# Top-1 routing: tokens routed at the start of the step behind their choice, and one sequence routed in two halves

## The chip, the cores and the metric

The kernel runs on one core of a Trainium2 chip. The metric is the device time of one execution in microseconds (us), the median of several runs. TensorE is called PE here, VectorE DVE, ScalarE ACT, GpSimd POOL and SyncE SP.

## The reference

The program computes attention with a local window and a few global keys, and sends its output as tokens through a layer of eight experts, of which each token uses one.

```python
# attention: B=4 sequences, H=8 heads, S=768 tokens, D=64; n_global=8, n_local=96
scores = q @ k.T / sqrt(D) - slope[h] * dist        # kept where local or global, else -1e9
a = exp(scores - max); a = a / (sum(a) + 1e-9)
x = (a @ v) as (B*S, H*D)                           # 3072 tokens x 512
# experts: E=8, w1 512x1024, w2 1024x512
logits = x @ w_gate; e = argmax(logits); p = softmax(logits)[e]
out[token] = p * (relu(x[token] @ w1[e]) @ w2[e])
```

## The kernel before, in words

**Tiles and order.** A sequence has six blocks of 128 tokens (NBLK = 6), so there are N = 24 blocks. The attention is a software pipeline of 24 steps, steps(n). Step n computes the scores of block n, the values of block n - 1, the sums and transposes of block n - 2, and the division of block n - 3 by its sums. The program writes every engine's instructions down in the order of the Python calls; each engine works through its own list in order, and a recorder (class Flow) puts in the semaphore waits that the data need. There is no scheduler: what is called first stands first in its engine's queue.

**What a step holds**, with the lines of the profile:

- scores (PE, L491, 32 matmuls, 16 in a sequence's first block), into PSUM banks 0 to 3.
- weigh (DVE, L501, or L503 in a first block), twice: adds the bias to half of the scores. exponent (ACT, L509), twice. both (POOL, L515 or L517), twice: adds the two key tiles for the row sums, into one of three buffers es, and reads the exponent's buffer e, of which there are two.
- values (PE, L528, 32 matmuls) and the copy of its result (ACT, L531).
- sums (PE, L543, 24 small matmuls: row sums and router logits), copied by ACT (L545); tokens_x and tokens_u (PE, L550, L553): transposes that bring a block back to one token per partition.
- normal (DVE, L562 to L566: four operations) takes the reciprocal of the sums and makes the logits; rows (DVE, L571) writes the tokens.
- q_in and k_in (PE, L475, L467): transposes of the tiles for step n + 2, copied by ACT (L477, L469). k_in writes bank 3, which weigh of the second half reads.
- copies of the global keys and values over the first rows of an older tile (POOL, L1096 and L1152, in step 22 ACT, L1094 and L1120).

**Routing.** When a sequence's six blocks have logits, at the end of steps 8, 14 and 20, choose (DVE, L584 to L588, and an exponent of ACT, L589) finds each token's expert, and gates (DVE, L594 to L598) its weight. In the next step counts (PE, L605 to L610: twelve small matmuls with a triangle and with ones) counts ahead of each token those of the same expert, and slots (DVE, L618 to L623) makes of it the token's row in a DRAM buffer, xg_dram, that has a region for each expert. base_e carries the counts on from sequence to sequence. Each block's tokens then go to their rows in one indirect DMA that POOL issues (scatter, L627). The calls wait in a list, scat; at the end of every step one is taken from it, and in the last sequence, from its fourth block on, all that are left (six, in step 21). The fourth sequence is routed later, inside the first group of the experts.

**Behind it.** At the end of step 21, load_x(0) loads expert 0's rows of the first three sequences (SP, L779 and L788); it waits until these sequences' scatters have landed. early_counts (DVE, L733 to L743 and three more) fixes expert 0's number of rows and so the form of its matmuls. marks and x_in (DVE, L795, L806) use what load_x brought. The experts' matmuls (PE, L842) follow; their up and down products use seven block products instead of eight, and w_sums (DVE, L710 to L713) makes the sums of weights that this takes: eight operations for expert 0, one at the end of each step from 13 to 20.

Of the kernel before, what the change touches and what calls it, by code (L numbers as in the profile page):

```python
# [15 lines left out]
I32 = mybir.dt.int32  # L16
AF = mybir.ActivationFunctionType
ALU = mybir.AluOpType
AX = mybir.AxisListType
# [305 lines left out]
class Attention:  # L325
# [9 lines left out]
    GW, LW, P, E = 32, 97, 128, 8  # L335
# [238 lines left out]
                            ALU.mult)  # L574


    def choose(self, b):

        f, k, V = self.f, self.keep, self.f.dve
        xr, lg = self.xr[b % 2], self.lg[b % 2]  # L580
        shape = [128, self.NBLK, self.E]
        sh, cand = self.small[:, 0], self.small[:, 1]
        top = self.top
        V.tensor_reduce(top, lg, AX.X, ALU.max)  # L584
        V.tensor_tensor(sh, lg, top.unsqueeze(2).to_broadcast(shape), ALU.subtract)
        V.scalar_tensor_tensor(cand, sh, 0.0, k["rev8"][:].unsqueeze(1).to_broadcast(shape), ALU.is_ge, ALU.mult)
        V.tensor_reduce(top, cand, AX.X, ALU.max)
        V.tensor_tensor(k["oh"][:], cand, top.unsqueeze(2).to_broadcast(shape), ALU.is_equal)  # L588
        f.act.activation(sh, sh, AF.Exp)  # L589

    def gates(self, b):
        f, k, V = self.f, self.keep, self.f.dve
        xr, sh, se = self.xr[b % 2], self.small[:, 0], self.se
# [3 lines left out]
        V.tensor_copy(out=xr[:, :, 513:514].bitcast(I32), in_=k["tokid"][:].unsqueeze(2))  # L597
        V.tensor_scalar(k["tokid"][:], k["tokid"][:], self.S, None, ALU.add)  # L598

    def counts(self, bank):  # L600
        f, k, E, NB = self.f, self.keep, self.E, self.NBLK
        oh, n = k["oh"], self.NBLK * self.E
        flat = oh[:].rearrange("p u e -> p (u e)")
# [9 lines left out]
    def slots(self, b, bank):  # L613
        f, k, V, E = self.f, self.keep, self.f.dve, self.E
        n = self.NBLK * E
        pr = self.psum[:, bank, 384:384 + n + E]
        rk = self.small[:, 2]
        V.tensor_tensor(rk, pr[:, 0:n].rearrange("p (u e) -> p u e", e=E),  # L618
                        k["base_e"][:].unsqueeze(1).to_broadcast([128, self.NBLK, E]), ALU.add)
        V.tensor_tensor(k["base_e"][:], k["base_e"][:], pr[:, n:n + E], ALU.add)  # L620
        V.tensor_tensor(rk, rk, k["oh"][:], ALU.mult)
        V.tensor_reduce(self.slot, rk, AX.X, ALU.add)
        V.tensor_copy(out=k["slot_i"][:, b % 2, :], in_=self.slot)  # L623

    def scatter(self, b, u):
        k = self.keep
# [8 lines left out]
class Experts:  # L635
# [10 lines left out]
    P, E, CAP, LATE, COMMON = 128, 8, 512, 128, 208  # L646
# [329 lines left out]
def kernel(  # L976
# [26 lines left out]
    NB = NTOK // P - 1  # L1003
# [24 lines left out]
    ident, iota_p, col, before, ones, rev8, ebase, base_e, tokid = (  # L1028
        keep[nm] for nm in ("ident", "iota_p", "col", "before", "ones", "rev8", "ebase", "base_e", "tokid"))
# [7 lines left out]
    with ExitStack() as stack:  # L1037
# [6 lines left out]
        f = Flow(tc)  # L1044
# [5 lines left out]
        N, V = at.N, f.dve  # L1050
        O, U, T0, T1, SK = 4, 5, 6, 7, 3
# [14 lines left out]
        at.loads(3)  # L1066

        scat, routed = [], {}
        tokens = [[f"xs{b}.{u}" for u in range(NBLK)] for b in range(B)]
        w0 = ex.w_pieces(0)  # L1070
        w0_sums = ex.w_sums(0, True) + ex.w_sums(0, False)
# [15 lines left out]
        def steps(n):  # L1087
            b, i = divmod(n, NBLK)
            at.scores(n)
            if i < NBLK - 1 and i >= 1:  # L1090

                first_k = at.kt[n % 3][:, :, 0:32], at.kg
                if n == N - 2:
                    f.act.copy(*first_k)  # L1094
                else:
                    f.pool.tensor_copy(out=first_k[0], in_=first_k[1])  # L1096
            if n >= 5 and w0:
                w0.pop(0)()
            if n == 0:
                kk, qq = at.k_in(1, O), at.q_in(1, U)  # L1100
                f.pool.tensor_copy(out=at.kg, in_=at.kt[0][:, :, 0:32])
            if n + 4 < N:
                at.loads(n + 4)
            if n + 3 < N:
                at.load_v(n + 3)
            at.weigh(n, 0)
            at.exponent(n, 0)
            if n == 0:
                kk()
                qq()  # L1110
            if n >= 3:
                at.normal(n - 3, U)
            first_v = None
            if n >= 1:
                values_part(n)
                bb, ii = divmod(n - 1, NBLK)
                if 1 <= ii < NBLK - 1:
                    first_v = at.v[(n - 1) % 6][0:32].rearrange("p h d -> p (h d)"), at.vg[bb % 2]
                    if n == N - 2:
                        f.act.copy(*first_v)  # L1120
            if n - 4 in routed:
                at.counts(T1)
# [18 lines left out]
            if n + 2 < N:  # L1141
# [12 lines left out]
            if us:  # L1154
                us()
                at.tokens_u(n - 2, U)
            if kk:
                qq()
                kk()
                if (n + 2) % NBLK == 0:  # L1160
                    f.pool.tensor_copy(out=at.kg, in_=at.kt[(n + 2) % 3][:, :, 0:32])
            if n == 1:
                V.tensor_scalar(before[:], col[:], iota_p[:, 0:1], None, ALU.is_gt)
                V.memset(ones[:], 1.0)
                V.tensor_copy(out=base_e[:], in_=ebase[:])
# [73 lines left out]
        def group(p):  # L1239
# [6 lines left out]
            def at_(i, *fns):  # L1246
                todo.setdefault(i, []).extend(fns)
# [41 lines left out]
            if g == 0:  # L1289
# [4 lines left out]
                pieces = ex.w_pieces(1)  # L1294
# [7 lines left out]
                        fn()  # L1302
                    ex.load_x(1, last)

                at_(2, lambda: at.normal(N - 1, U), lambda: at.choose(B - 1), *pieces[4:])
                at_(4, lambda: at.counts(U), lambda: at.gates(B - 1))
                at_(5, lambda: at.slots(B - 1, U))
# [468 lines left out]
```

## Time and profile before

| What | Value |
|---|---|
| Median of 3 runs | 517.89 us (516.78 to 520.77) |
| The profiled execution's own time | 517.95 us |
| Its span, first to last instruction | 516.1 us |
| Mean granted clock of PE | 0.985 |
| PE busy from step 20's values to step 22's scores (134.36 to 148.38 us) | 13.30 us |
| PE busy from step 22's values to step 23's scores (148.38 to 161.94 us) | 8.81 us, granted clock 0.77 |
| Indirect DMAs of L627, issue time | 24, mean 1030 ns |

The busy times come from a table of stretches: each row gives a stretch's length, then for each engine its busy time and the number of its instructions, then PE's granted clock, the share of the DMA engines' time and the rate in GB/s. A line of a timeline gives the start, the length, the engine, the line of the program, the operation, what it writes and reads, how many are merged, and, in brackets, how long the engine stood idle before it and what ended that. In a list of waits the numbers are the total in us, how often, and the longest.

Single scatters start at 71.8 us (end of step 9) and follow one per step until 139.4 us; six stand together at 147.6 to 155.1 us, and six more, those of the fourth sequence, at 182.9 to 190.7 us.

### The profile page before, as it was taken

The numbers are of one execution on the slowest core, as the hardware profiler recorded it, in microseconds if no ns is written. First come the engines' busy times: TensorE is split into PE (matmuls) and PEld (weight loads), VectorE is DVE, ScalarE is ACT, GpSimd is POOL, SyncE is SP. The second block draws the span as 40 slices with busy tenths as digits, with TensorE's granted clock in tenths as the row PEclk, the third lists the DMA queues.
The fourth block names the chain that finished last, engine by engine and source line by source line (L and its number), as shares of the span: only waits on it lengthen the run. The fifth ranks groups of instructions, "written<-read, shape, count | busy, mean of one in ns | idle before, by whom it ended". The sixth has DMA issues, their size and how long they took to land. (4 is left out here: it accounts for less than half of the span.)

```text
span 516.1 us, 10775 instructions
## 1 busy us (share of the span) xinstructions
PE 478.7 (93%) x4397; PEld 451.3 (87%) x4397; DVE 352.5 (68%) x626; ACT 174.1 (34%) x306; POOL 166.0 (32%) x192
## 2 busy tenths in 40 slices
PE   3999999999977999999998999997999999999980
PEld 3888888888866899999998999997999999999980
DVE  4654775897873884666775885865877667687840
ACT  3766555555543230323122223212204203303410
POOL 1554465667664053330024016006006103003011
PEclk9999999999997999999999999999999999999996
DMA  9999999998424437897783774656368378001000
GB/s 152 205 242 244 183 238 245 241 224 187 103 99 110 161 127 165 210 244 175 162 222 116 159 211 117 144 186 164 75 176 219 101 181 228 7 1 48 18 25 29
DMA packets 120344, 79.24 MB, mean 154 GB/s; under 512 B 86422, under 2 KB 103318, under 8 KB 120272
## 3 DMA queue, kind: packets, MB, share of 16 engines
q1 hardware_dynamic: 112960, 63.77, 55.9%
q0 software_dynamic: 6480, 14.45, 8.0%
q8 instruction: 51, 0.84, 0.7%
q14 instruction: 21, 0.17, 0.1%
q10 hardware_dynamic: 832, 0.02, 0.1%
HBM read 61.39 MB, written 23.71 MB: 165 GB/s over the span
## 5 line engine op out<-in xcount | busy, mean ns | idle before, releaser
L842 PE MATMUL psum<-arena 128*128 128x208 f32 (+5 forms) x1776 | 293.4, 325 | 8.1 <-ACT arena L870 6.5
L842 PEld LDWEIGHTS psum<-arena 128*128 128x128 f32 x1776 | 285.1, 190 | 12.6 <-ACT arena L870 8.0
L832 POOL DMA_INDIRECT out_dram<-arena,to x16 | 21.8, 1365 | 218.5 <-ACT arena L824 193.8
L501 DVE TENSOR_TENSOR arena<-psum,arena 128x1024 f32<-128x1024 f32 x40 | 48.8, 1219 | 37.2 <-PE psum L491 37.2
L515 POOL TENSOR_TENSOR arena<-arena 128x512 f32<-128x512 f32 x40 | 53.4, 1334 | 35.9 <-ACT arena L509 35.9
L509 ACT ACTIVATE arena<-arena 128x1024 f32<-128x1024 f32 (+1 forms) x48 | 47.4, 987 | 47.7 <-DVE arena L501 36.1
L491 PE MATMUL psum<-arena 64*128 64x128 f32 x704 | 50.2, 291 | 1.2 <-ACT arena L477 0.7
L866 ACT ACTIVATE arena<-arena 128x512 f32<-128x512 f32 x48 | 30.2, 630 | 61.2 <-DVE arena L901 30.8
L491 PEld LDWEIGHTS psum<-arena 64*128 64x128 f32 x704 | 45.0, 197 | 5.9 <-issue 3.4
L528 PE MATMUL psum<-arena 128*64 128x128 f32 x704 | 43.9, 277 | 0.2 <-issue 0.2
L870 ACT COPY arena<-psum 128x512 f32<-128x512 f32 (+1 forms) x24 | 13.5, 561 | 84.8 <-PE psum L842 83.2
L528 PEld LDWEIGHTS psum<-arena 128*64 128x64 f32 x704 | 38.2, 137 | 3.3 <-issue 0.6
L627 POOL DMA_INDIRECT xg_dram<-arena,slot_i x24 | 24.7, 1030 | 23.3 <-DVE arena L911 15.8
L911 DVE TENSOR_TENSOR arena<-arena,psum 128x512 f32<-128x512 f32 x24 | 16.5, 689 | 21.9 <-PE psum L842 18.3
L885 DVE TENSOR_TENSOR arena<-arena,psum 128x512 f32<-128x512 f32 (+1 forms) x24 | 15.8, 659 | 22.0 <-PE psum L842 20.7
L755 POOL DMA_INDIRECT xg_dram<-small,pad x24 | 25.7, 1070 | 12.5 <-issue 7.0
L906 DVE TENSOR_TENSOR arena<-arena,psum 128x512 f32<-128x512 f32 x24 | 16.5, 688 | 15.9 <-PE psum L842 14.2
L901 DVE TENSOR_TENSOR arena<-arena,psum 128x512 f32<-128x512 f32 x24 | 16.5, 688 | 14.8 <-PE psum L842 13.6
L467 PE MATMUL psum<-ident,arena 128*128 128x128 f32 x96 | 16.1, 294 | 8.7 <-DMA arena<-in_k_dram 7.1
L832 POOL DMA_INDIRECT out_dram<-ylast,to x17 | 17.4, 1025 | 20.6 <-ACT ylast L824 12.7
L874 DVE TENSOR_TENSOR arena<-arena,psum 128x512 f32<-128x512 f32 (+1 forms) x24 | 15.8, 656 | 11.0 <-PE psum L842 9.8
L713 DVE TENSOR_TENSOR arena<-arena 128x1024 f32<-128x1024 f32 x16 | 19.9, 1243 | 3.0 <-issue 2.9
(152 smaller groups left out, 535.2 us busy)
## 6 DMA issues: line engine op xcount, KB each, us to landing
arena<-in_moe_w_dram SPq DMA_DIRECT2D x64, 512.0 KB
arena<-xg_dram SPq DMA_DIRECT2D x64, 128.0 KB
arena<-in_q_dram SPq DMA_DIRECT2D x24, 256.0 KB
arena<-in_k_dram SPq DMA_DIRECT2D x24, 256.0 KB
arena<-in_v_dram SPq DMA_DIRECT2D x24, 256.0 KB
xg_dram<-arena SPq DMA_DIRECT2D x2, 1032.0 KB
xg_dram<-arena,slot_i POOLq DMA_INDIRECT x24
xg_dram<-small,pad POOLq DMA_INDIRECT x24
```

Source lines behind the costliest of these rows:

```text
L491: f.pe.matmul(self.psum[:, 2 * g + a, c:c + P], lhsT=kt[r, m, :], rhs=qt[r, m, :], start=True, stop=True, skip_group_check=True)
L501: f.dve.tensor_tensor(e, s, self.bias[:, g, :, 1:3, :].rearrange("p h k c -> p h (k c)"), ALU.add)
L509: f.act.activation(e, e, AF.Exp)
L515: f.pool.tensor_tensor(self.es[n % 3][:, g], e[:, :, 0:P], e[:, :, P:2 * P], ALU.add)
L528: f.pe.matmul(po[r, m, :], lhsT=self.v[(n - ab) % 6][:, 2 * m + a, :], rhs=self.e[n % 2][:, m // 2, 2 * a + m % 2, P * ab:P * ab + P], sta ...
L627: self.f.pool.indirect_dma_start(out=self.xs[:], out_offset=bass.IndirectOffsetOnAxis(ap=k["slot_i"][:, b % 2, u:u + 1], axis=0), in_=self ...
L713: lambda: V.tensor_tensor(c["t4"], c["b21"], c["t2"], ALU.subtract)]
L755: self.f.pool.indirect_dma_start(out=self.xs[:], out_offset=bass.IndirectOffsetOnAxis(ap=self.keep["pad"][:, g, j:j + 1], axis=0), in_=sel ...
L832: return pool.indirect_dma_start(out=self.out[:], out_offset=bass.IndirectOffsetOnAxis(ap=self.keep["to"][:, g, j:j + 1], axis=0), in_=sel ...
L842: f.pe.matmul(self.psum[:, bank, 256 * t + cut.start:256 * t + cut.stop], lhsT=w[k][:, ts(t, 128)], rhs=x[k][:, cut], start=(fresh and t = ...
L866: f.act.activation(d, d, act)
L901: V.tensor_tensor(dst["c22"], u3, bank(W), ALU.add)
```

## The change: what it does

- choose, gates, counts and slots take a slice of blocks, us, and work on that part of their buffers.
- A table, units, says behind which block a set is chosen. The first two sequences are sets of six blocks as before. The third (B - 2) is two sets of three: the first is chosen at the end of step 17, the second at the end of step 20.
- In the step behind the choice, normal, counts and slots stand ahead of the first weigh. Before, normal stood behind it, counts behind values, and slots behind rows.
- Step 21 issues all scatters that are in the list after values, ahead of the second weigh and of both halves of both(), with the copy of the global values moved ahead of them. Elsewhere one scatter is taken per step as before.
- early_counts goes from step 21 to step 22. q_in stands ahead of k_in in every step (in a routing step it stood behind tokens_x).
- Expert 0's weight sums start at step 12 and leave out the steps with a choice: 12, 13, 15, 16, 18, 19, 21 and 22.

```diff
@@ choose, gates, counts, slots: a slice of blocks, for instance
-    def choose(self, b):
+    def choose(self, b, us):
-        xr, lg = self.xr[b % 2], self.lg[b % 2]
-        shape = [128, self.NBLK, self.E]
+        lg = self.lg[b % 2][:, us]
+        shape = [128, us.stop - us.start, self.E]
...
-        V.tensor_tensor(k["oh"][:], cand, top.unsqueeze(2).to_broadcast(shape), ALU.is_equal)
+        V.tensor_tensor(k["oh"][:, us], cand, top.unsqueeze(2).to_broadcast(shape), ALU.is_equal)
...
@@ the main function
+        whole, half = slice(0, NBLK), NBLK // 2
+        units = {NBLK * b + NBLK - 1: (b, whole) for b in range(B - 2)}
+        units[NBLK * (B - 2) + half - 1] = B - 2, slice(0, half)
+        units[NBLK * (B - 2) + NBLK - 1] = B - 2, slice(half, NBLK)
...
@@ steps(n)
+            unit = routed.pop(n - 4, None)
+            if unit:
+                at.normal(n - 3, U)
+                at.counts(T1, unit[1])
+                at.slots(*unit, T1)
+                scat.extend((unit[0], u) for u in range(unit[1].start, unit[1].stop))
             at.weigh(n, 0)
             at.exponent(n, 0)
...
-            if n >= 3:
+            if n >= 3 and not unit:
                 at.normal(n - 3, U)
...
+                    if n == N - 3:
+                        f.pool.tensor_copy(out=first_v[0], in_=first_v[1])
-            if n - 4 in routed:
-                at.counts(T1)
+            if n == N - 3:
+                for s in scat:
+                    at.scatter(*s)
+                scat.clear()
             at.weigh(n, 1)
             at.exponent(n, 1)
-            bb = routed.pop(n - 4, None)
...
-            if bb is not None:
-                at.slots(bb, T1)
-                scat.extend((bb, u) for u in range(NBLK))
             us = at.sums(n - 2, U) if n >= 2 else None
-            if bb == B - 2:
+            if n == N - 2:
                 early_counts()
-            if n + 2 < N and bb is None:
+            if n + 2 < N:
                 qq = at.q_in(n + 2, T1)
...
-            if n + 2 < N and bb is not None:
-                qq = at.q_in(n + 2, T1)
...
-                if first_v and n != N - 2:
+                if first_v and n not in (N - 3, N - 2):
                     f.pool.tensor_copy(out=first_v[0], in_=first_v[1])
...
-            if n >= 3 and (n - 3) % NBLK == NBLK - 1:
-                at.choose((n - 3) // NBLK)
-                at.gates((n - 3) // NBLK)
-                routed[n - 3] = (n - 3) // NBLK
-            if n >= 13 and w0_sums:
+            if n - 3 in units:
+                unit = routed[n - 3] = units[n - 3]
+                at.choose(*unit)
+                at.gates(*unit)
+            elif n >= 12 and w0_sums:
                 w0_sums.pop(0)()
-            for _ in range(NBLK if b == B - 1 and i >= 3 else 1):
-                if scat:
-                    at.scatter(*scat.pop(0))
+            if scat:
+                at.scatter(*scat.pop(0))
```

More of the change, by code (lines that the diff above doesn't have):

```diff
@@ L574, in rows @@
                             ALU.mult)
-    def choose(self, b):
+    def choose(self, b, us):
         f, k, V = self.f, self.keep, self.f.dve
-        xr, lg = self.xr[b % 2], self.lg[b % 2]
-        shape = [128, self.NBLK, self.E]
-        sh, cand = self.small[:, 0], self.small[:, 1]
-        top = self.top
+        lg = self.lg[b % 2][:, us]
+        shape = [128, us.stop - us.start, self.E]
+        sh, cand = self.small[:, 0, us], self.small[:, 1, us]
+        top = self.top[:, us]
         V.tensor_reduce(top, lg, AX.X, ALU.max)
@@ L587, in choose, with gates @@
         V.tensor_reduce(top, cand, AX.X, ALU.max)
-        V.tensor_tensor(k["oh"][:], cand, top.unsqueeze(2).to_broadcast(shape), ALU.is_equal)
+        V.tensor_tensor(k["oh"][:, us], cand, top.unsqueeze(2).to_broadcast(shape), ALU.is_equal)
         f.act.activation(sh, sh, AF.Exp)
-    def gates(self, b):
+    def gates(self, b, us):
         f, k, V = self.f, self.keep, self.f.dve
-        xr, sh, se = self.xr[b % 2], self.small[:, 0], self.se
+        xr, sh, se, tokid = self.xr[b % 2][:, us], self.small[:, 0, us], self.se[:, us], k["tokid"][:, us]
         V.tensor_reduce(se, sh, AX.X, ALU.add)
@@ L596, in gates, with counts @@
         V.reciprocal(xr[:, :, 512:513], se.unsqueeze(2))
[L597 to L603, printed above, removed]
+        V.tensor_copy(out=xr[:, :, 513:514].bitcast(I32), in_=tokid.unsqueeze(2))
+        V.tensor_scalar(tokid, tokid, self.S, None, ALU.add)
+    def counts(self, bank, us):
+        f, k, E, NB = self.f, self.keep, self.E, us.stop - us.start
+        oh, n = k["oh"][:, us], NB * self.E
+        flat = oh.rearrange("p u e -> p (u e)")
         pr = self.psum[:, bank, 384:384 + n + E]
@@ L611, in counts, with slots @@
                         stop=(u == NB - 1), skip_group_check=True)
-    def slots(self, b, bank):
+    def slots(self, b, us, bank):
         f, k, V, E = self.f, self.keep, self.f.dve, self.E
-        n = self.NBLK * E
+        n = (us.stop - us.start) * E
         pr = self.psum[:, bank, 384:384 + n + E]
-        rk = self.small[:, 2]
+        rk = self.small[:, 2, us]
         V.tensor_tensor(rk, pr[:, 0:n].rearrange("p (u e) -> p u e", e=E),
-                        k["base_e"][:].unsqueeze(1).to_broadcast([128, self.NBLK, E]), ALU.add)
+                        k["base_e"][:].unsqueeze(1).to_broadcast([128, us.stop - us.start, E]), ALU.add)
         V.tensor_tensor(k["base_e"][:], k["base_e"][:], pr[:, n:n + E], ALU.add)
-        V.tensor_tensor(rk, rk, k["oh"][:], ALU.mult)
-        V.tensor_reduce(self.slot, rk, AX.X, ALU.add)
-        V.tensor_copy(out=k["slot_i"][:, b % 2, :], in_=self.slot)
+        V.tensor_tensor(rk, rk, k["oh"][:, us], ALU.mult)
+        V.tensor_reduce(self.slot[:, us], rk, AX.X, ALU.add)
+        V.tensor_copy(out=k["slot_i"][:, b % 2, us], in_=self.slot[:, us])
     def scatter(self, b, u):
@@ L1131, in steps @@
                 at.rows(n - 3, T0)
-            if bb is not None:
-                at.slots(bb, T1)
-                scat.extend((bb, u) for u in range(NBLK))
             us = at.sums(n - 2, U) if n >= 2 else None
-            if bb == B - 2:
+            if n == N - 2:
                 early_counts()
             kk = qq = None
-            if n + 2 < N and bb is None:
+            if n + 2 < N:
                 qq = at.q_in(n + 2, T1)
-            if n + 2 < N:
                 kk = at.k_in(n + 2, SK)
@@ L1303, in scatters @@
                     ex.load_x(1, last)
-                at_(2, lambda: at.normal(N - 1, U), lambda: at.choose(B - 1), *pieces[4:])
-                at_(4, lambda: at.counts(U), lambda: at.gates(B - 1))
-                at_(5, lambda: at.slots(B - 1, U))
+                at_(2, lambda: at.normal(N - 1, U), lambda: at.choose(B - 1, whole), *pieces[4:])
+                at_(4, lambda: at.counts(U, whole), lambda: at.gates(B - 1, whole))
+                at_(5, lambda: at.slots(B - 1, whole, U))
                 at_(6, lambda: at.rows(N - 1, T0), scatters)
```

## The prediction

> **What bounds the kernel now.** I read the page first, for the shares:
>
> ```profile
> span 516.1 us, 10775 instructions
> PE 478.7 (93%) x4397; PEld 451.3 (87%) x4397; DVE 352.5 (68%) x626; ACT 174.1 (34%) x306; POOL 166.0 (32%) x192
> ```
>
> TensorE (PE) is busy for 93%, so a gain must come from a stretch where PE stands, and every PE delay lasts to the end. Next, the waits in 140 to 170 us, the stretch of the changed routing (columns: us in total, times, longest):
>
> ```profile
> POOL arena L515 <- ACT arena L509: 8.6, 5, 3.8
> DVE arena L501 <- PE psum L491: 8.4, 1, 8.4
> ...
> ACT arena L531 <- remote: 5.2, 1, 5.2
> ...
> PE psum L553 <- ACT arena L545: 3.1, 2, 2.7
> ```
>
> One wait of 8.4 us is the largest hole of the attention part. Third, the timeline there, PE and POOL:
>
> ```profile
> 147.64 1.01 POOL L627 DMA_INDIRECT xg_dram<-arena,slot_i  x1 [0.81 <-DVE ki L740]
> ...
> 148.38 1.97 PE L528 MATMUL psum<-arena 128*64 128x128 f32 x32
> ...
> 153.41 0.29 PE L543 MATMUL psum<-arena 128*32 128x128 f32 x1 [0.44 <-issue]
> ...
> 154.12 0.98 POOL L627 DMA_INDIRECT xg_dram<-arena,slot_i  x1 [0.30 <-issue]
> ...
> 155.57 0.59 ACT L531 COPY arena<-psum 128x512 f32<-128x512 f32 x1 [5.15 <-remote]
> ...
> 157.82 0.47 PE L553 MATMUL psum<-ident,arena 128*128 128x128 f32 x1 [2.72 <-ACT arena L545]
> 158.23 3.79 PE L491 MATMUL psum<-arena 64*128 64x128 f32 x32
> ```
>
> POOL issues six scatters back to back (147.64 to 155.10). From the third on, PE creeps: the 24 matmuls of sums() take 150.28 to 153.70 instead of about 0.9 us, and ACT, which waits for values() (end shown at 150.35), starts only at 155.57. Then PE's clock is halved:
>
> ```profile
> 156.00:158.00 2.00, 0.18 (x1) 0.18 (x1) 0.00 (x0) 1.77 (x4) 0.70 (x2) 0.50 0.17 66
> 158.00:162.00 4.00, 4.00 (x35) 3.55 (x35) 1.57 (x4) 0.39 (x1) 0.96 (x1) 0.50 0.96 211
> ```
>
> (last columns: granted clock, DMA share, GB/s.) Scores take 3.79 us instead of 2.06. Is the burst the cause? The only other long "remote" wait on a compute engine says so; DVE waited for a matmul just behind a row of eight such issues of POOL, the last at 357.87:
>
> ```profile
> 360.22 0.69 DVE L911 TENSOR_TENSOR arena<-arena,psum 128x512 f32<-128x512 f32 x1 [2.89 <-remote]
> ```
>
> Against it: the six scatters at 182.9 to 190.7 show nothing alike; but PE then issues one matmul per 0.15 us, against one per 0.06 in attention.
>
> Price of the hole: without it, step 22's ACT chain would be exponent, L531 at 150.45, L1120, exponent, L545 ending near 152.7, and PE's scores of step 23 would start near 153.0 instead of 158.23 (5.2 us); half clock then costs 3.79 - 2.06 = 1.7 us and a little more. About 7.1 us in all.
>
> **What the skill says.** "TensorE: Matmul & The Clock Gate", Part 1: after an idle window of about 3.4 us PE falls to half clock. The trace agrees: half clock stands from about 155.6 to 162.4, 6.8 us, after PE's near-standstill. "Perfetto Trace Analysis", Summary: TensorE's end is estimated, and the window of a POOL DMA is descriptor generation only; so the 150.35 is no proof that PE had delivered. "SBUF — State Buffer", Who interferes with whom: VectorE and GpSimd share a port pair, PE and ACT wait for no one. The first half shows: L588 takes 0.94 us and L623 1.15 beside POOL, 0.21 and 0.17 alone (177.92, 181.91). The second half doesn't explain the hole above. "DMA: Bandwidth & Descriptors", Anatomy of one DMA: about 2 us to completion; here SP's load behind the sixth scatter starts at 157.07, 1.97 after its issue ends.
>
> **The change part by part.** The sum is against the profiled execution (517.95 us, span 516.1), which stands at the median (517.89).
>
> *Scatters.* The halving looks as if only three were left for step 21. Counting the queue gives six still: batch 1 fills it with six at step 15 and one leaves per step; at step 18 three are left, three new ones come behind, and steps 18 to 20 empty only batch 1's. Step 21 then issues all six in one go, as the built program shows (three, one with a wait on DVE, two). They move from behind both() of step 21 to ahead of it, behind the first_v copy, which waits for values(20). I place PE's values(20) at 141.0 to 142.9 and the copy's end at 143.6; the burst then is 143.7 to 151.3 (5 x 1.29 + 0.98 + the first's wait), about 4 us earlier, plus the routing cost below: 144.9 to 152.5. Behind it on POOL stand both() of step 21 (2 x 1.28, done near 155.1); sums(21) needs it in step 23, after 157, and weigh of step 23 needs its first half (153.8) near 154.2. Just hidden; a burst later by over 0.4 us shows one for one.
>
> *Routing ahead of weigh.* normal (four operations, 0.93 us) only moves. slots (0.95 us alone, 181.13 to 182.08) now waits for counts, which wait for scores; behind it on DVE queue both weigh; for these wait ACT's exponents, L545, then PE's tokens_u. Step 9: gates end 65.07, normal 66.0, counts done about 66.05, slots 67.0, weigh 68.15 and 69.25; ACT: exponent 69.3, L531 69.8, exponent 70.8, L545 71.05; tokens_u 71.05 instead of 70.08: +1.0, less 0.2 because scores then no longer run stretched (2.28 against 2.06). +0.8. Step 15: one weight sum (1.22 us at 102.04) leaves ahead of it, so weigh ends 106.35 as before (106.32): 0, less the same 0.2. Step 21: likewise, -0.1. Step 18 (new, half size; no row of before, so bounded by the full chain's 2.7 us and, at no less than 0.13 us each, some 1.5): choose and gates 119.65 to 122.2, normal 123.1, slots 124.05, weigh 125.25, ACT's chain 126.65, tokens_u 126.75 instead of 126.12: +0.65, the six counts (0.3) within it; with the short chain they alone remain, +0.3. Sum +1.2 us (bounds 0.3 to 2.0: below nothing is excluded only by PE's own matmuls).
>
> *Moved at no cost.* Weight sums at 12, 13, 15, 16, 18, 19, 21, 22 lie in DVE's idle time (3.07 us at 89.58, 8.43 at 160.36); without that, 1.22 each. Early counts (ten operations, 1.3 us) go to step 22, where DVE is idle from 151.9.
>
> *load_x(0).* SP issues it behind the sixth scatter: near 154.5 instead of 157.07; landed 6.5 us later (163.6 before), 161. marks and x_in need it at 167.8 now, or 161.8 if PE's hole vanished. Hidden; no gain.
>
> **Likeliest: the hole moves with the burst.** The burst now starts while PE waits for DVE and ACT (few matmuls from 145 to 147.4), so I let PE get through step 22's scores before it creeps, from 149.5 to 153.1. Then, half clock: values 157, sums 158, L545 158.7, scores of step 23 159.1 to 161.5, against 161.94: -0.4. At full clock, values 155.1, tokens_u 157, scores to 159.3: -2.7. If the creep begins with scores unfinished, +2.3. I take +0.6: **518.5 us**, own range 516 to 521.
>
> **Rivals.** *The hole vanishes* (its cause sat in step 22, or PE is idle enough): -7.1 + 1.2 = -5.9, 512.0. For it: no hole at 182.9. Against it: still six issues. *Slower:* the creep takes the scores of step 22 from the third scatter (147.5) to 153.1: 0.4 longer than now; half clock then lies wholly on PE-bound work (3.4 instead of 1.9: +1.5), and step 22's 0.8 us of slack on PE is gone; with routing 1.2: +3.9, 521.8, and 523.5 if the clock needs a further window (1.7). It decides if the creep begins before 149.5. For it and against it: PE had issued 60 matmuls from the burst's start to the creep (147.64 to 150.65); from 145 to the end of step 22's scores there are some 20 and 32, just fewer. *The change does nothing to routing's place:* excluded, the built order shows it.
>
> **How the numbers follow.** Hole moves 0.54; vanishes 0.24 (0.19 of it below 512.7); slower 0.22 (0.12 of it above 523.1). About 1% is what a measurement of this kernel can tell from no change. So faster 0.19, within 1% 0.69, slower 0.12. Range 511.5 to 523.5.
>
> **What would show it.** Right: six L627 in a row near 145 to 152.5, a stretched PE and a "remote" wait in their second half, half clock about 6.8 us behind it, PE about 0.8 late after step 9. Wrong: no half clock before 170 us (then 512), three L627 only in step 21, load_x as the wait of L795, or POOL's both() as the wait of weigh in step 23.

## The result and the profile after

The changed kernel takes 511.3 us in the median (509.54 to 515.73, 5 runs) beside 517.89 us of the kernel before (516.26 to 520.77, 5 runs): ratio 0.9891, 95% interval 0.985 to 0.9932. The forecast was 518.5 us; its range began at 511.5. On another chip, later, the same pair was level (0.9993, below), so the 1.1% is not a property of the program alone. Two of the eleven runs of the kernel before on the second chip, slow ones at over 1.5% above its fastest, are left out of its median below.

The page of the kernel after, first line and shares:

```profile
span 509.2 us, 10793 instructions
...
PE 476.8 (94%) x4397; PEld 449.5 (88%) x4397; DVE 358.0 (70%) x641; ACT 173.2 (34%) x307; POOL 167.3 (33%) x192
```

The span is 6.9 us shorter, with 15 VectorE instructions more. The timeline around the burst (lines of other instructions left out):

```profile
144.10 0.99 POOL L627 DMA_INDIRECT xg_dram<-arena,slot_i  x1 [0.16 <-issue]
...
150.51 1.10 PE L543 MATMUL psum<-arena,small 128*32 128x128 f32 x14
...
151.53 0.99 POOL L627 DMA_INDIRECT xg_dram<-arena,slot_i  x1 [0.30 <-issue]
...
151.95 5.55 DVE L734 TENSOR_SCALAR inv_i<-inv 128x4 int32<-128x4 f32 x1
...
152.53 4.94 POOL L515 TENSOR_TENSOR arena<-arena 128x512 f32<-128x512 f32 x4
...
153.51 0.59 ACT L531 COPY arena<-psum 128x512 f32<-128x512 f32 x1 [3.36 <-remote]
...
156.02 3.39 PE L491 MATMUL psum<-arena 64*128 64x128 f32 x32
```

Six scatters still stand in a row in step 21, 144.1 to 152.5 as forecast. The hole is at the same instructions as before, the sums of step 22 (L543), and L531 still waits for "remote" (the trace names no instruction that released it), 3.36 us where it was 5.15. Half clock follows; the table of stretches of the kernel after (stretch, length, busy time of PE, PEld, DVE, ACT, POOL, granted clock, DMA share, GB/s):

```profile
157.00:160.00 3.00, 3.00 (x32) 2.78 (x30) 2.86 (x9) 0.00 (x0) 0.47 (x1) 0.52 0.98 226
160.00:162.00 2.00, 2.00 (x50) 1.83 (x49) 1.90 (x6) 1.31 (x2) 0.18 (x1) 1.00 1.22 174
```

It lasts 3.41 us instead of 6.83. A new thing stands beside it: DVE's L734, an operation on 128 x 4 elements, takes 5.55 us while four of POOL's L515 run back to back. At PE's first expert matmul, before and after, only 1.7 us are gained:

```profile
169.78 1.89 PE L842 MATMUL psum<-arena 128*128 128x256 f32 x8
```

```profile
168.09 1.89 PE L842 MATMUL psum<-arena 128*128 128x256 f32 x8
```

The other 5.2 us come after it. PE's waits from 170 to 500 us, before:

```profile
PE psum L842 <- ACT arena L870: 6.5, 4, 3.5
```

and after:

```profile
PE psum L842 <- issue: 1.3, 3, 0.6
PE psum L842 <- ACT arena L870: 0.9, 1, 0.9
```

The reader is to see the place: the change touches the attention part, and three quarters of the gain sit among the experts, whose instructions are the same.

One table carries what follows. "Attention" is the time from PE's 60th matmul (near 17 us) to its 2,400th (in expert 0); "experts" from there to the 4,300th (480 to 490 us). On the first three chips the kernel before takes 513 to 518 us in the median; below they are said to stall. On the other three it takes 508 to 509 us.

| Execution | Span, us | Attention | Experts |
|---|---|---|---|
| before | 516.1 | 164.1 | 308.5 |
| after | 509.2 | 162.7 | 303.2 |
| before again, second chip | 512.3 | 162.6 | 306.0 |
| after again, second chip | 508.0 | 163.2 | 301.3 |
| before + 15 VectorE copies, third chip | 508.1 | 163.6 | 301.0 |
| after, burst put back, third chip | 506.5 | 163.5 | 299.4 |
| after, scatters spread 2-2-2, third chip | 507.3 | 160.0 | 303.3 |
| before, fourth chip | 505.8 | 162.7 | 299.6 |
| before + 15 copies, fifth chip | 507.3 | 163.9 | 299.6 |
| after, fifth chip | 506.4 | 163.4 | 299.5 |
| after, scatters spread 3-3-0, fourth chip | 504.5 | 161.2 | 299.2 |

299.2 to 299.8 us is the floor of the experts' part: the ten profiled executions on the last three chips, six programs, lie there. What stands above it is waiting, and half clock behind the waits.

### The profile page after: what moved, and what is told of

Its sections match the earlier page's. It is cut to its first block, busy times and chain, and to the rows that moved or that the text cites. A ratio compares the mean times of both kernels' runs of the same rounds, so it can differ in the third digit from the quotient of the medians.

```text
span 509.2 us, 10793 instructions
## 1 busy us (share of the span) xinstructions
PE 476.8 (94%) x4397; PEld 449.5 (88%) x4397; DVE 358.0 (70%) x641; ACT 173.2 (34%) x307; POOL 167.3 (33%) x192
## 5 line engine op out<-in xcount | busy, mean ns | idle before, releaser
L842 PE MATMUL psum<-arena 128*128 128x208 f32 (+5 forms) x1776 | 292.3, 325 | 3.2 <-issue 1.3
L842 PEld LDWEIGHTS psum<-arena 128*128 128x128 f32 x1776 | 285.3, 190 | 6.5 <-issue 2.2
L515 POOL TENSOR_TENSOR arena<-arena 128x512 f32<-128x512 f32 x40 | 52.5, 1316 | 32.9 <-ACT arena L509 32.8
L491 PE MATMUL psum<-arena 64*128 64x128 f32 x704 | 49.0, 288 | 1.9 <-ACT arena L469 1.2
L491 PEld LDWEIGHTS psum<-arena 64*128 64x128 f32 x704 | 43.9, 195 | 6.2 <-issue 2.5
L870 ACT COPY arena<-psum 128x512 f32<-128x512 f32 (+1 forms) x24 | 13.5, 561 | 83.6 <-PE psum L842 83.5
L627 POOL DMA_INDIRECT xg_dram<-arena,slot_i x24 | 25.5, 1061 | 21.4 <-DVE arena L911 16.0
## 6 DMA issues: line engine op xcount, KB each, us to landing
arena<-in_moe_w_dram SPq DMA_DIRECT2D x64, 512.0 KB
```

Of the source, the lines that this page charges most:

```text
L491: f.pe.matmul(self.psum[:, 2 * g + a, c:c + P], lhsT=kt[r, m, :], rhs=qt[r, m, :], start=True, stop=True, skip_group_check=True)
L515: f.pool.tensor_tensor(self.es[n % 3][:, g], e[:, :, 0:P], e[:, :, P:2 * P], ALU.add)
L627: self.f.pool.indirect_dma_start(out=self.xs[:], out_offset=bass.IndirectOffsetOnAxis(ap=k["slot_i"][:, b % 2, u:u + 1], axis=0), in_=self ...
L842: f.pe.matmul(self.psum[:, bank, 256 * t + cut.start:256 * t + cut.stop], lhsT=w[k][:, ts(t, 128)], rhs=x[k][:, cut], start=(fresh and t = ...
```

## The experiments

My theory A for the hole: PE's small matmuls and their signals are held up while POOL issues a row of indirect DMAs. Rival B: it is PE's own instruction fetch at that place. For the experts' gain, once it was seen, theory C: VectorE's fetches had fallen into POOL's rows and no longer do. Rival D: chance, of the chip or the moment.

### Both kernels again, and with 64 idle matmuls

The kernel before and the changed one on a second chip, one execution each; and both with 128 more instructions of PE in step 12, which moves all later fetches by half a block. The product of the idle matmuls is not used.

```diff
+            if n == 12:
+                for _ in range(64):
+                    f.pe.matmul(psum[:, O, 0:8], lhsT=before[:], rhs=ones[:, 0:8], start=True, stop=True,
+                                skip_group_check=True)
             if n >= 1:
                 values_part(n)
```

> The kernel before, unchanged, for a second profile. If the creep of PE during the six scatters belongs to the program, ACT's L531 of step 22 waits about 5 us again and half clock follows (about 7 us lost in the attention part), and the time is 516 to 521 us. If it was one execution's accident, this wait is missing. The two long waits of PE in the experts' part (2.6 us near 277, 3.8 us near 358) show whether they stand at the same places again (then the 5.2 us that the changed kernel won behind the attention part belong to the change) or not (then these are chance).

> The changed kernel, unchanged, for a second profile: 509 to 516 us. In its first profile L531 of step 22 waited 3.4 us and half clock lasted 3.4 us instead of 6.8; if the shorter hole belongs to the change it is again between 3 and 4 us, first matmul of the experts near 168.1 us. If the gain in the experts' part belongs to the change, PE's waits there are again under 1 us each.

> The kernel before with 64 tiny matmuls (8 columns, bf16, about 0.03 us each, about 2 us in all) added in step 12; their result is overwritten. They put 128 more PE instructions ahead of step 22. Theory A (a row of scatters alone slows PE, from the third on): the hole stays where the burst is, at the sums of step 22, and the time is 517.9 + 2 = 520 us. Theory B (PE's instructions arrive in 16 KB blocks over a DMA queue of their own; in both kernels the creep begins at the same PE instruction, some 25 ahead of a new block, and the scatters hold up that block): the block now changes about 4 us earlier, before the burst, so L531 of step 22 doesn't wait, no half clock before 170 us, 517.9 + 2 - 7 = 513 us.

> The changed kernel with the same 64 tiny matmuls in step 12. Theory A: the hole stays at the sums of step 22 as in the changed kernel, 511.3 + 2 = 513 us. Theory B: the block now changes near the start of step 22's scores, within the burst (which began at 144.1 and sent its data from about 145 on), so the creep moves to those scores; if the burst is too young there to hold the block up, it is gone: 513 - 4 = 509 us.

Measured: before 514.18, after 509.87 (one execution each; before's median on that chip 512.87, nine runs). With 64 idle matmuls, before takes 528.88 (ratio 1.0313, 1.0263 to 1.0363), after 520.76 (1.0161, 1.0116 to 1.0206). The idle matmuls themselves make 2.5 and 2.8 us (scores of step 14 in these traces, beside those without them). In both the hole stays at step 22's sums (L531 waits from 152.84 to 157.21 and from 153.23 to 156.43), though PE's fetch near it moved from 151.6 to 149.1 in the kernel before. So B falls for this hole. But two new holes stand among the experts, in both kernels. PE's waits, 170 to 500 us, of before with 64 idle matmuls:

```profile
PE psum L842 <- issue: 10.0, 2, 5.3
PE psum L842 <- ACT arena L870: 1.9, 2, 1.4
```

and the timeline there:

```profile
227.78 4.39 PE L842 MATMUL psum<-arena 128*128 128x208 f32 x24
236.86 3.48 PE L842 MATMUL psum<-arena 128*128 128x208 f32 x9 [4.69 <-issue]
```

PE waited for nothing but its own issue. The trace has a packet of the instruction queue at 234.2, inside a row of POOL's DMAs, and the same at 283.6. Each is followed by 6.83 us of half clock; in the changed kernel the two waits are 2.71 and 4.88 us, with 3.41 us of half clock behind each. The Trainium skill, "Runtime: NRT & Kernel Launch", Instruction fetch mechanics, says that an engine fetches its program in 16 KiB blocks of 256 instructions over a DMA queue of its own. The trace agrees for PE (51 packets of 16 KB, 194 to 310 PE records apart in the straight code of the attention part). The page takes the cost of such a block as mostly hidden; at these two places it seems not to be. A row alone does not do it: in the kernel before, packets of PE stand inside rows of five to eight DMAs at 232.3, 273.0, 312.5 and 354.3 us, and no L842 waits for its issue. What sets the two apart is not shown.

### Spread, 15 copies, a whole block of PE, the burst put back

Third chip, where the kernel before took 514.29 us. The changed kernel with two scatters per step in steps 18 to 20, so that three are left for step 21:

```diff
-            if scat:
-                at.scatter(*scat.pop(0))
+            for _ in range(2 if n in (18, 19, 20) else 1):
+                if scat:
+                    at.scatter(*scat.pop(0))
```

> The changed kernel with two scatters instead of one at the end of steps 18, 19 and 20, so that only the three of the last half are left to be issued in a row in step 21. Theory A (the hole at the sums of step 22 comes from small matmuls that run while GpSimd issues a row of at least four or five indirect DMAs): no hole there; ACT's L531 of step 22 starts within 0.6 us of the end of values() at about 150.4 instead of 3.2 to 3.4 us behind it, no half clock in 150 to 165 us, the first experts' matmul near 164 instead of 168.1 and 168.6, total about 505 to 508. Rival B (TensorE's own instruction block at this place makes the hole): hole as before, first experts' matmul at 168 to 169, total about 510 to 511. Rival A2 (three are already enough): a hole of 1 to 2 us, first experts' matmul near 166.5.

Measured: 506.84 us, ratio 0.9856 (0.9827 to 0.9885), the lowest of all programs on a chip that stalls. The hole of step 22 is gone, and there is no half clock until the tail. Timeline of the spread kernel:

```profile
143.52 0.18 DVE L618 TENSOR_TENSOR small<-psum,base_e 128x24 f32<-128x24 f32 x1 [1.26 <-remote]
...
152.60 0.59 ACT L531 COPY arena<-psum 128x512 f32<-128x512 f32 x1 [0.47 <-PE psum L528]
```

L531 follows PE as it should. With the six back in one row, on the same chip (the last program of this part; waits of 138 to 172 us), it waits again:

```profile
ACT arena L531 <- remote: 4.0, 1, 4.0
```

So on this chip the row of six makes the hole, as A says; on the chips without stalls, below, the same row makes none. How a row holds PE up is not shown. The attention part gains 2.7 to 3.2 us, and not the 4.1 to 4.6 expected. A smaller stall now stands in step 21, where L618 waits for the counts. Two scatters (140.73 and 142.04) and a fetch of PE (142.2) stand beside it; that their meeting makes it was not tested on a chip that stalls.

The kernel before with 15 tiny VectorE copies, the number of VectorE instructions that the change adds:

```diff
+            if n == 12:
+                for _ in range(15):
+                    V.tensor_copy(out=keep["cnt"][:, 1:2], in_=base_e[:, 1:2])
```

> The kernel before with 15 tiny VectorE copies at the end of step 12, where VectorE has time to spare: VectorE then has as many instructions ahead of the experts as in the changed kernel, and nothing else is touched. Theory C (the gain in the experts' part comes from VectorE's instruction blocks that are fetched at other places): the waits of TensorE's L842 for ACT's L870 sink from 6.5 and 3.9 to 1 us or less, and the total sinks by 2.5 to 5 us to about 509 to 511. Rival (the gain there comes from what the order of the work does to the experts' phase, or from chance): waits and total as before, 512.5 to 516, ratio 0.995 to 1.005.

Measured: 510.96 us, ratio 0.994 (0.9915 to 0.9964). Its attention part is that of before (163.6; L531 waits 4.3 us for "remote"). PE's waits of 170 to 500 us:

```profile
PE psum L842 <- DVE arena L874: 0.8, 1, 0.8
PE psum L842 <- ACT arena L870: 0.6, 2, 0.4
```

The waits for L870 are short (there is no trace of the kernel before on this chip; on the first two they were 6.5 and 3.9 us). Timeline of PE in the third row of experts' DMAs, before (first chip):

```profile
351.67 6.92 PE L842 MATMUL psum<-arena 128*128 128x208 f32 x42
362.10 4.16 PE L842 MATMUL psum<-arena 128*128 128x184 f32 x25 [3.51 <-ACT arena L870]
```

and before with 15 copies:

```profile
349.75 14.50 PE L842 MATMUL psum<-arena 128*128 128x184 f32 x90
```

Ninety matmuls without a gap. What 15 instructions of 2.3 us in an idle place moved is VectorE's fetches: the trace shows packets of 8 KB (its queue q14) after 188, 316 and 450 VectorE instructions in the kernel before. DMA queues of the kernel before, 266 to 280 us, around POOL's row of eight issues from 267.15:

```profile
q0 software_dynamic: 640, 1.15, 23.8%
q8 instruction: 1, 0.02, 0.5%
q14 instruction: 1, 0.01, 0.3%
```

and of before with 15 copies, 267 to 280 us, around the same row, which starts at 266.86:

```profile
q0 software_dynamic: 640, 1.15, 25.1%
q8 instruction: 1, 0.02, 0.5%
```

The q14 packet is out of the row: 254.5 us instead of 269.0. At the third row it is 344.2, half a microsecond ahead of the row, instead of 350.1 inside it. The changed kernel has them at 254.0 and 343.8. This is what C says of the places. How a late packet of VectorE would hold PE up is not shown: in the kernel before, VectorE runs on behind the packet of 269.0, and what comes late, 10 us behind it, is a result of PE for ACT:

```profile
269.25 1.22 DVE L711 TENSOR_TENSOR arena<-arena 128x1024 f32<-128x1024 f32 x1
271.14 0.59 DVE L885 TENSOR_TENSOR arena<-arena,psum 128x416 f32<-128x416 f32 x1 [0.67 <-PE psum L842]
```

```profile
278.98 0.59 ACT L870 COPY arena<-psum 128x512 f32<-128x512 f32 x1 [1.51 <-remote]
```

Nor does a packet in a row bring the long wait each time. In the kernel before with 64 idle matmuls, on the second chip, both packets stood inside the rows (279.0 and 365.4), and L870's waits were 1.9 us in all, the longest 1.4.

The kernel before with 128 idle matmuls, a whole block of PE:

> The kernel before with 128 idle matmuls in step 12: 256 instructions of TensorE, one whole instruction block, so that the blocks change at the same places of the experts' part as without them. Block theory: the two holes of about 5 us that 64 idle matmuls opened in the experts' part (TensorE waiting for nothing but the issue of L842) are not there; the total is before plus the idle matmuls' own 5 to 8 us, 519 to 522. Rival (it is the later start of the experts' part that opens them): issue holes as with 64, total 530 to 535.

Measured: 523.26 us, ratio 1.0159 (1.0125 to 1.0193), and no wait of L842 for its issue over 0.8 us. The idle matmuls themselves make 7.9 us of the 9.0, with half clock from 88.4 to 95.2 us among them. So a later start does not open the two holes; the phase of PE's blocks is what is left, as far as two chips can be set side by side. One wait of 3.5 us for L870 is still there; VectorE's fetches here are still inside the rows (277.1 and 360.1), and the experts' part takes 306.9 us.

The changed kernel with step 21's six scatters back behind both():

```diff
-            if n == N - 3:
-                for s in scat:
-                    at.scatter(*s)
-                scat.clear()
             at.weigh(n, 1)
...
-            if scat:
-                at.scatter(*scat.pop(0))
+            for _ in range(6 if n == N - 3 else 1):
+                if scat:
+                    at.scatter(*scat.pop(0))
```

> The changed kernel with the six scatters of step 21 put back behind both() of step 21, as in the kernel before; all else as changed. If the burst's place matters for the hole: TensorE creeps in the sums of step 22 from about 151, L531 of step 22 waits 4.3 to 5.2 us instead of 3.4, the first experts' matmul comes 1 to 1.7 us later than in the changed kernel, or up to 2.7 later where VectorE's L734 doesn't get its 5.5 us back; total 511 to 514. If the row of scatters costs the same in both places: the same within 0.5 us. The experts' part, if the routing's other edits made its gain, stays as in the changed kernel (waits of L842 for ACT under 1.5 us); if the burst made it, they return to 4 to 6.5 us.

Measured: 510.38 us, ratio 0.9941 (0.9907 to 0.9975). L531 waits 4.0 us for "remote", the first expert matmul comes at 169.26, and the experts' part takes 299.4 us without a wait for L870. So the burst's place is not what cured the experts' part. And the time is that of the kernel before with 15 copies on the same chip (0.9941 and 0.994): here the rest of the change gives no more than 15 VectorE instructions do.

### Counter-tests for C, and a chip without stalls

If C holds, a whole block of 128 VectorE instructions must give nothing to the kernel before, and 113 more (15 + 113 = 128) must take the gain from the changed kernel. The copies became memsets that wait for nothing.

```diff
+            if 2 <= n < 12:
+                for j in range(11 + (3 if n == 11 else 0)):
+                    V.memset(keep["cnt"][:, 1 + j % 7:2 + j % 7], 0.0)
```

(12 and 8 in place of 11 and 3 for the 128.) Beside them, scatters spread three in step 18, three in 19 and none in 20, and the kernel before once more.

> The changed kernel with 113 tiny VectorE memsets spread over steps 2 to 11, so that VectorE has 15 + 113 = 128 instructions more than the kernel before ahead of the experts and its 8 KB fetches fall at the old places again (near 269 and 350 us instead of 254 and 344). Theory C (a VectorE fetch that falls into a row of GpSimd's indirect DMAs costs the experts' part its waits): waits of L842 for ACT's L870 back at 3 to 6.5 us, total 512 to 515 (the memsets themselves are put where VectorE waits, 0 to 1 us). Rival (the experts' gain comes from something else in the change, or from chance): waits at 1 us, total 509.5 to 511.5.

> The kernel before with 128 tiny VectorE memsets over steps 2 to 11, one whole block of 128: VectorE's fetches behind step 12 stay where they were. Theory C: no gain, ratio 0.998 to 1.004, waits of L842 for ACT's L870 of 3 to 6.5 us, unlike the 15 copies, which gave 0.994. Rival (any extra VectorE instruction, or chance, gives the same gain): ratio near 0.994, waits under 1.5 us.

> The changed kernel with three scatters at the end of step 18, three at the end of step 19, and none left for step 20, so that none is issued beside TensorE's instruction fetch of step 21 at 142 us; step 21 issues three as in the run that spread two per step. If scatters beside that fetch made the 1.6 us that TensorE stood in step 21 there: gone, the first experts' matmul at 164.0 to 164.5 instead of 165.7, total 505 to 506. Rival (the counts' tiny matmuls are what stalls, fetch or not): a wait of VectorE for the counts as before, total 506.5 to 508.

> The kernel before once more, for the places of its fetches and the waits of its experts' part. Theory C: a VectorE fetch near 268 and near 348 us, inside the rows of GpSimd's issues, and waits of L842 for ACT's L870 of 3 to 6.5 us, total 513 to 518. Rival (chance): waits anywhere between 0 and 6.5.

Measured, fourth chip: before 508.63 (33 runs; its profiled execution 507.69), with 128 memsets 508.99 (1.0003, 0.999 to 1.0015), after with 113 memsets 509.15 (1.0004, 0.9989 to 1.0018), spread 507.05 (0.9965, 0.9952 to 0.9977). The expectation for the kernel before, 513 to 518, missed: here no program stalls. The fetches were where C puts them (267.7 in before and 269.3 in both padded kernels, inside the row), and still nothing waited. So the counter-tests tell nothing here, but one thing is shown: a fetch of VectorE inside a row does not cost by itself. If it costs, it does so on some chips, or at some times, and not on others.

The same four programs of C on a fifth chip:

> The changed kernel once more, beside the three below on one chip. If the kernel before takes 513 us or more here (it stalls): ratio 0.987 to 0.993. If it takes about 508.5 as in the last call (no stalls): theory D gives a ratio of 0.998 to 1.003, since in the attention part the routing's own cost of 0.5 to 1.2 us stands against a slightly later or earlier burst; if it is still 0.99 there, the gain doesn't come from stalls.

> The kernel before with 15 tiny VectorE copies in step 12, as in the third call. Where before stalls: theory C gives 0.992 to 0.996; a rival by which the 0.994 was chance gives 0.998 to 1.003. Where before doesn't stall: 0.999 to 1.002 by both.

> The kernel before with 128 tiny VectorE memsets over steps 2 to 11. Where before stalls: theory C gives 0.998 to 1.003 with waits of L842 for ACT's L870 of 3 to 6.5 us; the rival (any extra instructions do it) gives 0.994. Where before doesn't stall: 1.000 as in the last call.

> The changed kernel with 113 tiny VectorE memsets over steps 2 to 11. Where before stalls: theory C gives a loss of half to all of the gain, 0.994 to 1.001, with waits of L842 for ACT's L870 of 3 to 6.5 us; the rival gives the changed kernel's ratio plus at most 0.002. Where before doesn't stall: 1.000 as in the last call.

Measured: before 508.61 (57 runs), after 508.42 (0.9993, 0.9984 to 1.0001), before with 15 copies 508.26 (0.999, 0.9982 to 0.9999), with 128 memsets 508.93 (1.0004, 0.9993 to 1.0014), after with 113 memsets 509.12 (1.0005, 0.9998 to 1.0013). No stalls again, and all five within 0.2%. Where nothing stalls, the change gives nothing that can be told.

The two counter-tests once more, sixth chip:

> The kernel before with 128 tiny VectorE memsets over steps 2 to 11. If before takes over 512 us on this chip (it stalls): theory C gives 0.998 to 1.003, with waits of L842 for ACT's L870 of 3 to 6.5 us; the rival (any extra VectorE instructions do it, or chance) gives about 0.994 and waits under 1.5 us. If before takes about 508.6: 1.000 again, and nothing is told apart.

> The changed kernel with 113 tiny VectorE memsets over steps 2 to 11. If before takes over 512 us on this chip: theory C gives 0.994 to 1.001, waits of L842 for ACT's L870 of 3 to 6.5 us; the rival gives 0.988 to 0.993. If before takes about 508.6: 1.0005 again.

Measured: 508.32 (1.0003, 0.9993 to 1.0012) and 508.96 (1.0004, 0.9993 to 1.0016) beside 508.33. No stalls: not told apart.

### What the change does where nothing stalls

These traces show the attention part undisturbed. Waits of the kernel before, fourth chip, 138 to 176 us:

```profile
DVE to L795 <- DMA gt<-xg_dram: 4.7, 1, 4.7
...
PE psum L842 <- DVE arena L806: 4.2, 1, 4.2
ACT arena L531 <- PE psum L528: 3.4, 2, 2.9
```

There is no "remote" wait, yet PE stands 4.2 us: with the hole gone, load_x(0) is late. The timeline of it:

```profile
165.10 0.16 DVE L795 TENSOR_TENSOR to<-gt,is_i 128x4 int32<-128x4 int32 x1 [4.71 <-DMA gt<-xg_dram]
...
166.78 3.53 PE L842 MATMUL psum<-arena 128*128 128x256 f32 x8 [4.22 <-DVE arena L806]
```

The kernel after, fifth chip:

```profile
152.35 5.56 DVE L734 TENSOR_SCALAR inv_i<-inv 128x4 int32<-128x4 f32 x1
...
152.91 4.96 POOL L515 TENSOR_TENSOR arena<-arena 128x512 f32<-128x512 f32 x4
...
161.68 1.08 PE L543 MATMUL psum<-arena,small 128*32 128x128 f32 x16 [4.19 <-DVE small L564]
```

The earlier burst does remove the wait for load_x. But POOL's both() piles up behind the burst, L734 takes 5.56 us beside it, and PE stands 4.19 us for VectorE in step 23. One wait of 4.2 us is traded for another of 4.2 us, each with its half clock. The Trainium skill, "SBUF — State Buffer", Who interferes with whom, has VectorE and GpSimd on one port pair; the trace agrees that the two collide: L734 ends 0.04 us behind POOL's row, and it takes 0.17 us (at 155.22) in the kernel spread 3-3-0. That spread escapes both waits (PE's wait for load_x is 0, and there is no half clock until the tail) and is the one version that is faster than before on both kinds of chip, as 2-2-2 on one and 3-3-0 on the other; neither was run on both.

## Why the prediction was wrong, step by step

- **The burst**: right. Six in a row, 144.10 to 152.52 for a forecast of 144.9 to 152.5, on the chips without stalls as well.
- **The routing's cost**, +1.2 us: too high. In every pair of traces step 9 gave +0.93 to +0.95 at the next step's scores, of which +0.71 stayed, for the forecast's +0.8. Step 15 gave about -0.25 for -0.2, step 18 +0.47 to +0.49 for +0.65, step 21 about -0.2 for -0.1. At step 22's scores +0.7 us are left, +0.9 in one pair (all from PE's 60th matmul).
- **The hole stays with the burst**: right in kind, in its place and its "remote" wait, and still the likeliest case. Wrong in size: -2.8 us at the hole for the forecast's -0.6 (+0.6 less 1.2), of which +1.0 was lost again to L734, which "DVE is idle from 151.9" had put down at nothing. The signs that the prediction named came out mixed: six L627, the remote wait, PE 0.9 late after step 9, but half clock of 3.41 us and not 6.8.
- **The price of the hole**, 7.1 us: it fell. Without stalls the hole isn't there, and the attention part of before takes 162.7 to 163.9 us instead of 162.6 to 164.1. The gain of a missing hole goes to load_x's wait. A step that failed here is "load_x(0) ... Hidden; no gain": its x data were said to be needed at 161.8 if the hole vanished and, for the changed kernel, to land at 161. That margin was worked out for the changed kernel only; for before, whose load came at 163.6 or later, the same line shows a wait. The price of 7.1 us leaves it out.
- **The step that failed**: the sum ended at step 23's scores, and with "every PE delay lasts to the end" it put all that comes behind, the experts' part, at nothing. No reason is given for that. "The only other long 'remote' wait on a compute engine", DVE's 2.89 us at 360.22, was read as evidence about the burst and never priced. It and the 6.5 us of L842's waits for L870 stood in the experts' part, whose instructions the change does not touch but whose waits moved. In the first pair -5.2 of -6.9 us come from there, in the second -4.7 of -4.3.
- **Why the experts' part gained**: shown is that 15 copies alone, with no change of the routing, take 0.6% off on a chip that stalls (0.994), and that two packets of VectorE left the rows there, with short waits for L870. With PE's blocks at their old phase, the experts' part took 308.5, 306.0 and 306.9 us on the three stalling chips in the three executions with VectorE's packets inside the rows, and 299.4 to 303.3 in the five with them ahead. So the places of VectorE's fetches go with the gain; that they cause it is argued, not shown. Against it stand the short waits with 64 idle matmuls and the 303.2 and 303.3 us, 3 to 4 us above the floor, with the packets ahead. What stays open: the two counter-tests met only chips without stalls, so that any other shift of VectorE's instructions, or a chance order of these eight, is not excluded. Why some chips stall and others don't is open too; each set of runs was on another chip, so chip and hour can't be separated. On the third chip the 15 copies gave as much as the change with the burst put back; the changed kernel itself was not run there, so whether 15 instructions explain all of the first chip's -1.1% is not known.
- **The rivals**: the time fell beside the rival "the hole vanishes", 512.0 us, but by luck and not by its mechanism: the hole stayed, and the gain came from elsewhere. Nothing of "slower" was seen on PE's scores of step 22; its idea of a wait that takes the place of the one removed is what the chips without stalls show, only with another engine (VectorE for POOL).
- **The chances**: 0.69 for "within 1%" holds on the fifth chip (0.9993), and "faster by over 1%", given 0.19, on the first. The range took the rows of POOL's DMAs for fixed costs of every execution; the executions' spread of the kernel before, 506.9 to 520.8 us over six chips, is wider than the range.

## What to carry to other kernels

An edit shifts the instruction stream of every engine it adds to, so read the waits behind the edit too, and price those that hang on a row of DMAs issued by GpSimd: here they came and went with 15 instructions, and with the chip. Before a hole is priced, ask what is late next in the unchanged kernel (here a load whose wait the hole had covered), and before a burst is moved, what piles up behind it on its own engine. Spreading the burst paid where moving it did not; a gain of 1% on one chip is to be measured on a second before it is believed.

## What was not expected of the hardware

- The same kernel took 517.9, 512.9 and 514.3 us in the median on three chips, with "remote" waits of ACT and DVE of up to 5.2 us in its traces of the first two, and 508.6, 508.6 and 508.3 on three others, without such waits in the one trace of it taken there (fourth chip).
- VectorE's program comes in packets of 8 KB, TensorE's in 16 KB. In the straight code of the attention part two VectorE packets stand 128 recorded instructions apart (after 188 and 316). The page cited above gives 16 KiB for each engine; the measurement decides for VectorE.
- With 64 idle matmuls (second chip) TensorE stood 4.69 and 5.30 us for its own issue where packets of its program fell inside rows of GpSimd's indirect DMAs, with 6.83 us of half clock behind each; other packets inside such rows brought no such wait.
- A VectorE operation on 128 x 4 elements took 5.55 us beside four GpSimd operations of 128 x 512 in a row: it ended within 0.05 us of the row's end, and so gave way to the whole row, not to one operation.
